# Second MLP layer of the last four token groups by Strassen's scheme, with gelu as one ScalarE instruction from group 7 on

## The chip, the cores and the metric

The kernel runs on one core of a Trainium2 chip. A core has five engines that run their own instruction streams in order and wait for each other on semaphores: TensorE (PE in the profile; its weight loads are shown apart as PEld), VectorE (DVE), ScalarE (ACT), GpSimd (POOL) and SyncE (SP), whose only work here is to issue transfers. The metric is the time of one execution on the device in microseconds. Before the change it is 345.12 us, the median of three runs (345.02 to 345.3).

## What is computed

An attention is followed by a two-layer MLP. For each of 8 batches and 8 heads there are 576 queries of 64 elements, and as many keys and values; 16 "beacon" keys and values stand before them. A query sees all beacon keys and, of the others, those up to its own place.

```
scores = 1/sqrt(64) * q @ concat(beacon_k, k).T     # causal mask on the k part
a      = softmax(scores)
attn   = a @ concat(beacon_v, v)
x      = attn, as 4608 tokens x 512                  # token = batch * 576 + place, heads side by side
h      = x @ w_in                                    # 512 x 2048
g      = h * sigmoid(1.702 * h)
out    = g @ w_out                                   # 2048 x 512, out is 4608 x 512 in float32
```

The kernel computes in float16 with float32 sums.

## The kernel before

**Attention.** The 64 pairs of batch and head are taken in 16 sets `s` of four heads of one batch (two sets a batch). `e_turn` (L353) brings q and k of a set into the layout in which the head's elements lie on the partitions, on VectorE. `e_qk` (L382) makes scores for a chunk of up to 512 columns for four heads at once, in a PSUM tile `s`; `e_exp` (L393) takes the exponential into the SBUF tile `E`; `e_mask` (L407 on VectorE, L414 on GpSimd) clears what is not seen; `e_zadd` (L445) adds up pieces of `E` for the row sums; `e_av` (L467) multiplies by the values, or by ones for the sums; `e_z1`, `e_z2` and `e_norm` (L478 to L496) divide and write `xT`, which here holds all 4608 tokens.

**MLP.** Tokens are cut into ten groups: groups 0 and 1 have 256 tokens, groups 2 to 9 have 512. In `e_m1` (L518) each of the 16 tiles of 128 columns of h takes four matmuls of 128x128 weights (of `w_in`) against the group's tokens, in one PSUM tile of a ring of four (`u0` to `u3`). `e_tanh` (L532, ScalarE) writes tanh(0.851 h) to `sig`, and `e_gate` (L539, VectorE) writes (sig + 1) * h to the tile `g`, which is twice the activation. In `e_m2` (L551) each of a group's four blocks of 128 tokens takes 16 matmuls, with a 128x128 block of `g` as the weights and 512 columns of `w_out` as the moving operand. `e_evac` (L565, ScalarE) halves the sum on its way to SBUF, and `e_store` (L571) writes 128 rows of 2 KB out from SP. The tile `g` has two buffers, so that the first layer of group g waits for the second layer of group g-2.

**Order.** Everything is issued in an order worked out ahead by `Plan` (L24): each piece of work is entered with an engine, an estimated duration, what it depends on, a priority `pr` (smaller first) and an earliest time `due`. `run` (L63) plays the engines forward and takes on each engine, but PE, the ready piece with the smallest (pr, ready time, sequence). On PE, `choose` (L137) takes scores first and then alternates first-layer and second-layer pieces, the lower group first. The engines then execute their streams in that order, whatever the real durations are. The chunks of scores are due at even distances between `T_ATT0` (11000 ns) and `T_ATT1` (245000 ns), so that MLP matmuls fill PE between them. A PSUM ring tile is free again when the piece that `closes` it is done (the gate for the first layer, the evacuation for the second).

Priorities on VectorE: exponent masks and divisions 0, gates 2, row-sum additions 3, transposes of q and k 4.

Of the kernel before, what the change touches and what calls it, by code (L numbers as in the profile page):

```python
# [162 lines left out]
def kernel(  # L163
# [37 lines left out]
    ep = ctx.enter_context(tc.tile_pool(name="ep", bufs=NE))  # L201
    zp = ctx.enter_context(tc.tile_pool(name="zp", bufs=2))
    gp = ctx.enter_context(tc.tile_pool(name="gp", bufs=2))
    sp = ctx.enter_context(tc.tile_pool(name="sp", bufs=3))
    pss = ctx.enter_context(tc.tile_pool(name="pss", bufs=1, space=bass.MemoryType.PSUM))
    psu = ctx.enter_context(tc.tile_pool(name="psu", bufs=1, space=bass.MemoryType.PSUM))
# [2 lines left out]
    ones = cst.tile([P, 32], F16, tag="ones", name="ones")  # L209
    w1t = cst.tile([P, NKT, DFF], F16, tag="w1", name="w1")  # L210
    w2t = cst.tile([P, NNT, DMODEL], F16, tag="w2", name="w2")
    xT = cst.tile([P, NKT, NTOK], F16, tag="xT", name="xT")
    bkf = cst.tile([P, NSET, D], F32, tag="bkf", name="bkf")
    bkn = cst.tile([P, 2, D], F16, tag="bkn", name="bkn")
    qn = [cst.tile([P, TR * D], F16, tag=f"qn{i}", name=f"qn{i}") for i in range(NB3)]
# [276 lines left out]

    def e_norm(s, x, half):
        b, hs = divmod(s, HS)
        t0 = b * S + half * HF
        nc.vector.tensor_tensor(  # L496
            out=xT[:, 2 * hs + x, t0 : t0 + HF],
            in0=rings[("av", s, x, half)][:, 0:HF],
            in1=zs[(s, half)][1][:, :],
            op=ALU.mult,  # L500
        )
# [7 lines left out]
    def e_m1(g, n0, n1):  # L509
        t0, t1 = GROUPS[g]  # L510
        w = t1 - t0
        if n0 == 0:
            gts[g] = gp.tile([P, NNT, 512], F16, tag="g", name="g")
        u = ring_tile(("m1", g, n0))
        for nt in range(n0, n1):
            o = (nt - n0) * w
            for kp in range(NKT):
                nc.tensor.matmul(  # L518
                    u[:, o : o + w],
                    w1t[:, kp, nt * P : (nt + 1) * P],  # L520
                    xT[:, kp, t0:t1],
                    start=(kp == 0),
                    stop=(kp == NKT - 1),
                )

    sigs = {}

    def e_tanh(g, n0, n1):
        w = (GROUPS[g][1] - GROUPS[g][0]) * (n1 - n0)
        sig = sp.tile([P, 512], F16, tag="sig", name="sig")  # L530
        sigs[(g, n0)] = sig
        nc.scalar.activation(  # L532
            out=sig[:, 0:w], in_=rings[("m1", g, n0)][:, 0:w], func=AFT.Tanh, scale=0.851
        )

    def e_gate(g, n0, n1):
        w = GROUPS[g][1] - GROUPS[g][0]
# [20 lines left out]

    osbs = {}

    def e_evac(g, mt, eng):
        osb = sp.tile([P, DMODEL], F32, tag="osb", name="osb")
        osbs[(g, mt)] = osb
        if eng == "ACT":
            nc.scalar.mul(out=osb[:, :], in_=rings[("m2", g, mt)][:, :], mul=0.5)  # L565
        else:
            nc.vector.tensor_scalar_mul(osb[:, :], rings[("m2", g, mt)][:, :], 0.5)

    def e_store(g, mt):
        t0 = GROUPS[g][0] + mt * P  # L570
        nc.sync.dma_start(out=out[t0 : t0 + P, :], in_=osbs[(g, mt)][:, :])  # L571


    T_ATT0, T_ATT1 = 11000, 245000
    NCH0 = 4 * HS
    T_CH = (T_ATT1 - T_ATT0) / (len(CHUNKS) - NCH0)

# [12 lines left out]
        return flight[-1]  # L590

    op = plan.op
    turn, qks, exps, masks, avs, norms = {}, {}, {}, {}, {}, {}
    vload = {}
    gates, m2s = {}, {}
# [35 lines left out]
    def turns(s):  # L631
        urgent = s < HS
        cast = op(
            "DVE", 80, ld_bk[s] + [turn.get((s - 2, 1))], lambda: e_bk(s),
            pr=0 if urgent else 4, due=max(8800 * s if s < HS else 26000, due_of(s) - 10000), name=f"bk{s}",
        )
        for which in (1, 0):
            deps = [ld_qk[(s, which)], cast if which else None]
            turn[(s, which)] = op(
                "DVE", 1095 + 140 * which, deps + [qks[i] for i in CH_OF.get(s - NB2, [])],  # L640
                lambda which=which: e_turn(s, which),
                pr=0 if urgent else 4, due=max(0, due_of(s) - 9000), name=f"turn{s}",
            )
# [35 lines left out]
    def values(s):  # L679
        b, hs = divmod(s, HS)  # L680
        whole = s >= ZSUM
        order = [(2, 1), (2, 0), (0, 0), (1, 0), (0, 1), (1, 1)] if whole else [
            (x, h) for h in range(2) for x in (2, 0, 1)
        ]
        sums, z2 = [], {}
        if whole:
            for i, w in enumerate((ZW, HF - s0s[2], HF, HF, S - s0s[3], S - s0s[4])):
                if i in (0, 2):
                    cols = [(ecol[i], ecol[i] + HF), (ecol[i + 1], ecol[i + 1] + HF)]
                    if i == 0:  # L690
                        cols = [(Z0, HF), (ecol[1], ecol[2])]
                    else:
                        cols = [(ecol[3], ecol[4]), (ecol[4], ecol[5])]
                else:
                    k = 2 if i == 1 else i + 2
                    cols = [(ecol[k], ecol[k] + w)]
                sums.append(
                    op(
                        "DVE", 80 + 0.55 * 4 * w, [x for u, v in cols for x in after(s, u, v)] + sums[-1:],
                        lambda i=i: e_zadd(s, i), pr=3, name="zadd",  # L700
                    )
                )
        for n, (x, half) in enumerate(order):
            deps = after(s, 0, ETOT) if whole else after(s, half * EHALF, ETOT if half else EHALF)
            if x < 2:
                deps += [vload[(b, j)] for (j, _, _) in AVP[half]] + [vload[(b, -1)]]
                deps += [z2[h] for h in range(2) if whole]
                deps += [avs[(s, 2, half)]]
            w = [e - a for (_, a, e) in AVP[half]]
            if x == 2 and whole:  # L710
                deps += sums
                w = [HF] if half else [ZW, Z0 - 32, 32]
            key = ("av", s, x, half)
            avs[(s, x, half)] = op(
                "PE", sum(y / 2.4 + 6 for y in w), deps,
                lambda x=x, half=half: e_av(s, x, half), kind="av",
                pr=(16 * s + (n if whole else 8 * half)) if s >= HS else half,
                ring=key, mode="c", name=f"av{s}.{x}.{half}", tail=w[-1],
            )
            if x == 2:  # L720
                z1 = op("DVE", 410, [avs[(s, x, half)]], lambda h=half: e_z1(s, h), pr=0, closes=key, name="z1")
                z2[half] = op("DVE", 600, [z1], lambda h=half: e_z2(s, h), pr=0, name="z2")
            else:
                norms[(s, x, half)] = op(
                    "DVE", 380, [avs[(s, x, half)], z2[half]], lambda x=x, half=half: e_norm(s, x, half),
                    pr=1 if s >= HS else 0, closes=key, name="norm",
                )
# [34 lines left out]
    for j in range(-1, NJ):  # L762
        load_v(1, j)

    def mlp(g):
        t0, t1 = GROUPS[g]
        w = t1 - t0
        xs = []
        for hb in range(t0 // HF, (t1 - 1) // HF + 1):
            b, half = divmod(hb, 2)  # L770
            for hs in range(HS):
                for x in range(2):
                    xs.append(norms[(HS * b + hs, x, half)])
        old = [m2s[(g - 2, mt, 3)] for mt in range((GROUPS[g - 2][1] - GROUPS[g - 2][0]) // P)] if g > 1 else []
        n = 512 // w
        for n0 in range(0, NNT, n):
            n1 = n0 + n
            key = ("m1", g, n0)
            pe = op(
                "PE", 4 * n * (w / 2.4 + 2.5), xs + w1_of[n0] + old, lambda n0=n0, n1=n1: e_m1(g, n0, n1),  # L780
                kind="m1", pr=g, ring=key, mode="m", name=f"m1.{g}.{n0}",
            )
            a = op("ACT", 555, [pe], lambda n0=n0, n1=n1: e_tanh(g, n0, n1), pr=1, name="tanh")
            gates[(g, n0)] = op(
                "DVE", 610, [a], lambda n0=n0, n1=n1: e_gate(g, n0, n1), pr=2, closes=key, name="gate"
            )
        for mt in range(w // P):
            key = ("m2", g, mt)
            prev = None
            for qt in range(4):  # L790
                deps = [gates[(g, n0)] for n0 in range(0, NNT if mt else 4 * qt + 4, n)] + [w2_ld[qt], prev]
                prev = op(
                    "PE", 4 * 215.8, deps, lambda g=g, mt=mt, qt=qt: e_m2(g, mt, qt), kind="m2",
                    pr=g, ring=key, mode="m", name=f"m2.{g}.{mt}.{qt}",
                )
                m2s[(g, mt, qt)] = prev
            ev = op("ACT", 560, [prev], lambda g=g, mt=mt: e_evac(g, mt, "ACT"), pr=1, closes=key, name="evac")
            op("SP", 60, [ev], lambda g=g, mt=mt: e_store(g, mt), name="store")

    g = 0  # L800
    for i, ch in enumerate(CHUNKS):
# [11 lines left out]
        for s, c0, c1 in ch:  # L813
            if c1 == ETOT:
                values(s)
                while s % HS == HS - 1 and g < NG and GROUPS[g][1] <= (s // HS + 1) * S:
                    mlp(g)
                    g += 1
    order = plan.run()
    for o in order:  # L820
        o.emit()
# [29 lines left out]
```

## Time and profile before

| what | value |
|---|---|
| median of the runs | 345.12 us |
| the profiled execution: its own time, and its span from first to last instruction | 345.13 us, 343.4 us |
| granted TensorE clock over the span | 1.000 |
| busy time of PE, DVE, ACT, POOL | 324.2, 234.3, 203.6, 117.2 us |
| last exponential (L393) starts, takes | 242.62 us, 1.88 us |
| first-layer matmuls (L518): first and last start | 18.2 us, 325.6 us |
| second-layer matmuls (L551): first and last start | 30.2 us, 339.4 us |
| the last evacuation (L565) starts, takes | 339.85 us, 0.60 us |

Times within the profile count from the start of the span. A group's row gives a number of instructions, their busy time and the mean duration of one, and the idle time before them with the engine that ended it. Matmuls overlap in their pipeline, so the pace of a stream of them is read from the starts, not from the duration of one. A row of the timeline gives a start, the time from that start to the end of the last merged instruction, and how many were merged ("x4"). A row of the windows gives busy time by engine in a stretch, and in brackets how many instructions.

### The profile page before, as it was taken

To read this page: it belongs to the slowest core of one execution; us is meant where nothing else is said; L and a number is where in the kernel's file an instruction comes from. 1 tells how busy PE (TensorE), PEld (TensorE's weight loads), DVE (VectorE), ACT (ScalarE), POOL (GpSimd) and SP (SyncE) were. 2 spreads that over 40 slices of the span, in tenths; PEclk is the share of its full clock that TensorE was granted. 3 is DMA by queue.
4 is the path that set the end of the run, shared out by engine and by line. 5 is a ranking of instruction groups with operands and counts; after the bars stand their busy time and mean duration, and the time that the engine had idled before them with its cause. 6 is when DMAs were issued, how large, how long until landed. Compare 5 with 4: busy or idle time off the path is not lost.

```text
span 343.4 us, 9569 instructions
## 1 busy us (share of the span) xinstructions
PE 324.2 (94%) x4104; PEld 172.7 (50%) x4104; DVE 234.3 (68%) x454; ACT 203.6 (59%) x247; POOL 117.2 (34%) x190
## 2 busy tenths in 40 slices
PE   0699899999999999999999999999999999999995
PEld 0476666544554554555454545555444544444442
DVE  3856878499968798998888987987546444444400
ACT  1575587788547775776777676676643444444411
POOL 8765583394256329212653182231100000000000
PEclk9999999999999999999999999999999999999999
DMA  7999999694339149805093396000000000100021
GB/s 128 170 205 209 190 209 110 133 69 74 48 116 142 33 71 87 118 32 103 5 161 64 79 92 111 32 33 34 31 31 32 32 31 31 62 32 31 32 82 71
DMA packets 54122, 28.80 MB, mean 84 GB/s; under 512 B 41280, under 2 KB 45376, under 8 KB 54080
## 3 DMA queue, kind: packets, MB, share of 16 engines
q0 software_dynamic: 47552, 18.49, 46.0%
q1 hardware_dynamic: 6464, 9.69, 7.9%
q8 instruction: 32, 0.52, 0.6%
q14 instruction: 10, 0.08, 0.1%
q10 hardware_dynamic: 64, 0.01, 0.0%
HBM read 37.22 MB, written 9.44 MB: 136 GB/s over the span
## 4 chain that ended last, share of the span: by engine, by line
PE 75%; DVE 11%; issue 5%; POOL 3%; ACT 3%; DMA 2%; SPq 1%; DVEq 0%; POOLq 0%; ACTq 0%
PE u L551 33%; PE u L518 28%; PE u L467 7%; PE s L382 7%; ACT E L393 3%; DVE g L539 3%; DVE zs L445 2%; POOL E L414 2%; DMA bkf<-in_beacon_k_dram 2%; DVE qT L353 1%; DVE kT L353 1%; POOL vb L313 1%; DVE rz L487 1%; DVE zt L478 1%; DVE xT L496 1%
## 5 line engine op out<-in xcount | busy, mean ns | idle before, releaser
L518 PE MATMUL u<-xT,w 128*128 128x512 f16 (+1 forms) x640 | 145.7, 360 | 2.4 <-DVE g L539 1.1
L551 PE MATMUL u<-w,g 128*128 128x512 f16 x576 | 142.5, 379 | 0.0
L539 DVE SCALAR_TENSOR_TENSOR g<-sig,u 128x512 f16<-128x512 f16 x144 | 96.6, 681 | 64.0 <-ACT sig L532 63.2
L532 ACT ACTIVATE sig<-u 128x512 f16<-128x512 f32 x144 | 85.2, 598 | 86.5 <-PE u L518 84.0
L393 ACT ACTIVATE E<-s 128x2048 f16<-128x2048 f32 (+4 forms) x66 | 98.8, 1515 | 26.0 <-PE s L382 25.2
L414 POOL TENSOR_SCALAR_AFFINE_SELECT E<-E 128x512 f16<-128x512 f16 (+3 forms) x90 | 52.8, 612 | 118.3 <-ACT E L393 107.3
L518 PEld LDWEIGHTS <-w 128*128 128x128 f16 x640 | 60.7, 98 | 62.1 <-issue 2.9
L551 PEld LDWEIGHTS <-g 128*128 128x128 f16 x576 | 54.5, 98 | 63.4 <-issue 0.2
L382 PE MATMUL s<-qT,kT 32*128 32x32 f16 (+9 forms) x1544 | 36.0, 227 | 12.2 <-DVE qT L353 10.9
L382 PEld LDWEIGHTS <-kT 32*128 32x128 f16 x1544 | 28.5, 95 | 33.8 <-issue 21.4
L565 ACT ACTIVATE osb<-u 128x512 f32<-128x512 f32 x36 | 21.5, 597 | 22.3 <-PE u L551 22.3
L445 DVE TENSOR_TENSOR zs<-zs,E 128x192 f16<-128x192 f16 (+3 forms) x48 | 27.0, 563 | 4.6 <-ACT E L393 2.7
L467 PE MATMUL u<-E,vb 128*32 128x288 f16 (+4 forms) x1024 | 29.2, 258 | 0.8 <-DVE g L539 0.4
L496 DVE TENSOR_TENSOR xT<-u,rz 128x288 f16<-128x288 f32 x64 | 26.2, 448 | 4.1 <-PE u L467 3.7
L313 POOL DMA_DIRECT2D vb<-in_v_dram x32 | 27.2, 863 | 2.1 <-DMA qn<-in_q_dram 1.4
L467 PEld LDWEIGHTS <-vb 128*32 128x32 f16 (+1 forms) x1024 | 22.6, 98 | 4.6 <-issue 1.9
L353 DVE STREAM_TRANSPOSE kT<-kn 128x576 f32<-128x576 f32 x16 | 20.1, 1257 | 3.8 <-DMA kn<-in_k_dram 2.8
L353 DVE STREAM_TRANSPOSE qT<-qn 128x576 f32<-128x576 f32 x16 | 20.0, 1247 | 0.5 <-DMA qn<-in_q_dram 0.5
L445 DVE TENSOR_TENSOR zs<-E 128x704 f16<-128x704 f16 (+1 forms) x24 | 16.1, 671 | 5.4 <-POOL E L414 3.4
L478 DVE STREAM_TRANSPOSE zt<-u 128x288 f32<-128x288 f32 x32 | 14.0, 463 | 5.6 <-PE u L467 5.6
L487 DVE STREAM_TRANSPOSE rz<-rc 128x288 f32<-128x288 f32 x32 | 15.3, 478 | 1.1
L297 POOL DMA_DIRECT2D kn<-in_k_dram x16 | 9.1, 569 | 2.8 <-DVE g L539 2.0
(27 smaller groups left out, 66.8 us busy)
## 6 DMA issues: line engine op xcount, KB each, us to landing
out_dram<-osb SPq DMA_DIRECT2D x36, 256.0 KB, 2.0
kn<-in_k_dram POOLq DMA_DIRECT2D x16, 288.0 KB, 6.7
qn<-in_q_dram POOLq DMA_DIRECT2D x16, 288.0 KB, 6.3
vb<-in_v_dram POOLq DMA_DIRECT2D x24, 128.0 KB, 5.9
w<-in_moe_w_in_dram POOLq DMA_DIRECT2D x8, 256.0 KB, 9.0
w<-in_moe_w_out_dram POOLq DMA_DIRECT2D x4, 512.0 KB, 13.9
vb<-in_v_dram POOLq DMA_DIRECT2D x8, 112.0 KB, 3.3
vb<-in_v_dram POOLq DMA_DIRECT2D x8, 80.0 KB, 5.3
```

Source lines behind the costliest of these rows:

```text
L313: nc.gpsimd.dma_start(out=t[0 : hi - lo, j, h0:h1, :], in_=v[b, h0:h1, lo:hi, :].rearrange("h n d -> n h d"),)
L353: nc.vector.transpose(out=f32(dst.rearrange("p n e -> p (n e)")).rearrange("p (r t) -> p t r", t=TR), in_=f32(src[:, :]).rearrange("p (t c ...
L382: nc.tensor.matmul(sc[:, h, o : o + w], kT[s % NB2][r : r + 32, j * P : (j + 1) * P, d], qT[s % NB2][r : r + 32, a : a + w, d], start=(d = ...
L393: nc.scalar.activation(out=Es[s][:, :, c0:c1], in_=ss[i][:, :, o : o + c1 - c0], func=AFT.Exp, scale=0.125,)
L414: nc.gpsimd.affine_select(out=blk, in_=blk, compare_op=ALU.is_ge, fill=0.0, base=off + (Nb if j == 0 else 0), pattern=[[0, Q], [1, w]], ch ...
L445: nc.vector.tensor_tensor(out=t[:, :, o : o + w], in0=x, in1=y, op=ALU.add)
L467: nc.tensor.matmul(u[32 * h : 32 * h + 32, a:e], lhs, src[0:kw, h, col : col + e - a], start=first, stop=last,)
L496: nc.vector.tensor_tensor(out=xT[:, 2 * hs + x, t0 : t0 + HF], in0=rings[("av", s, x, half)][:, 0:HF], in1=zs[(s, half)][1][:, :], op=ALU. ...
L518: nc.tensor.matmul(u[:, o : o + w], w1t[:, kp, nt * P : (nt + 1) * P], xT[:, kp, t0:t1], start=(kp == 0), stop=(kp == NKT - 1),)
L532: nc.scalar.activation(out=sig[:, 0:w], in_=rings[("m1", g, n0)][:, 0:w], func=AFT.Tanh, scale=0.851)
L539: nc.vector.scalar_tensor_tensor(out=gts[g][:, n0:n1, 0:w], in0=sigs[(g, n0)][:, 0 : n * w].rearrange("p (n w) -> p n w", n=n), scalar=1.0 ...
L551: nc.tensor.matmul(o[:, :], gts[g][:, nt, mt * P : (mt + 1) * P], w2t[:, nt, :], start=(nt == 0), stop=(nt == NNT - 1),)
```

## The change

The change has five parts.

1. **Second layer of groups 6 to 9.** The product of a group, 512 tokens x 2048 by 2048 x 512, is taken as a product of 2 x 2 blocks (tokens in halves of 256, the 2048 in halves of 1024, output columns in halves of 256), by Winograd's form of Strassen's scheme: seven block products in place of eight. `e_prod` makes one of them: 8 x 2 matmuls of 128x128 weights against 256 columns, both token blocks in the halves of one ring tile, entered in four pieces of four matmuls.
2. **Sums on VectorE.** Four sums of blocks of `g` (`e_s`: three into the new tiles `sA`, one in place in `g`), each in four pieces of 128x512 elements of float16, wait for the gates (or gelus) they read and for all products of the group before, and have priority 2. Four sums of blocks of `w_out` (`e_t`, 128x2048 each, priority 3, from 200 us on) are made once; the fourth goes into the memory of `bkf`, after the last beacon key was read from it. The seven products are put together by one scaling on ScalarE (`e_half`) and seven instructions `e_join` on VectorE, and written out by four stores of 256 rows x 1 KB (`e_store4`).
3. **Gelu.** From group 7 on, one ScalarE instruction with the function `Gelu_apprx_sigmoid` takes the place of tanh and gate. The first one waits for all exponentials and for group 6's tanhs, the others wait for the first. These groups' outputs are not halved.
4. **`xT` as a ring** of 4 x 576 tokens in place of 4608. Values of a batch wait for the first layer of the groups whose places they overwrite; group 5 lies over the ring's end, and its first layer is issued in two parts of 256 tokens.
5. **Plan.** `T_ATT0`, `T_ATT1` become 13000 and 235000 ns. Output tiles come from a pool of their own, of four.

```diff
-    xT = cst.tile([P, NKT, NTOK], F16, tag="xT", name="xT")
+    XR = 4 * S
+    NPL, NPE, GEL = 6, 10, 7
+    HM, HN = 256, NNT // 2
+    xT = cst.tile([P, NKT, XR], F16, tag="xT", name="xT")
+    sA = [cst.tile([P, HN, HM], F16, tag=f"sA{i}", name=f"sA{i}") for i in range(3)]
+    tB = [cst.tile([P, HN, HM], F16, tag=f"tB{i}", name=f"tB{i}") for i in range(3)]
...
+            cut = max(t0, t1 // XR * XR)
+            for a, e in ((t0, cut), (cut, t1)):
+                for kp in range(NKT if a < e else 0):
+                    nc.tensor.matmul(
+                        u[:, o + a - t0 : o + e - t0],
+                        w1t[:, kp, nt * P : (nt + 1) * P],
+                        xT[:, kp, a % XR : (e - 1) % XR + 1],
...
+    def e_gelu(g, n0, n1):
...
+        nc.scalar.activation(
+            out=gts[g][:, n0:n1, 0:w],
+            in_=rings[("m1", g, n0)][:, 0 : n * w].rearrange("p (n w) -> p n w", n=n),
+            func=AFT.Gelu_apprx_sigmoid,
+        )
...
-    T_ATT0, T_ATT1 = 11000, 245000
+    def e_prod(g, p, n0, n1):
+        u = ring_tile(("p", g, p))
+        w = lambda i, j: w2t[:, HN * i : HN * (i + 1), HM * j : HM * (j + 1)]
+        lhs, rhs = {
+            1: (quarter(g, 0, 0), w(0, 0)),
+            2: (quarter(g, 0, 1), w(1, 0)),
+            3: (sA[2], w(1, 1)),
+            4: (quarter(g, 1, 1), tb(2)),
+            5: (sA[0], tb(0)),
+            6: (sA[1], tb(1)),
+            7: (quarter(g, 1, 0), tb(3)),
+        }[p]
+        for n in range(n0, n1):
+            for mt in range(2):
+                nc.tensor.matmul(
+                    u[:, HM * mt : HM * (mt + 1)],
+                    lhs[:, n, mt * P : (mt + 1) * P],
+                    rhs[:, n, :],
...
+    def e_join(g, p, src, dst):
...
+        nc.vector.scalar_tensor_tensor(
+            out=osbs[(g, dst)][:, :], in0=rings[("p", g, p)][:, :], scalar=scale_of(g), in1=osbs[(g, src)][:, :],
+            op0=ALU.mult, op1=ALU.add,
+        )
...
+    T_ATT0, T_ATT1 = 13000, 235000
...
+    SQ, SDVE, TDUE = 2, 0, 200000
+
+    def weights():
+        prev = []
+        for i in range(4):
+            prev = [op("DVE", 1450, w2_ld + prev, lambda i=i: e_t(i, "DVE"), pr=3, due=TDUE, name="t")]
+            tds[i] = prev[0]
...
+    def products(g):
+        eng = "POOL" if g < SDVE else "DVE"
+        sd = {}
+        for n0 in range(0, HN, SQ):
+            n1 = n0 + SQ
+            prev = []
+            for i in range(4):
+                deps = prev + done.get(g - 1, [])
+                for n in range(n0, n1):
+                    deps += [gates[(g, n)], gates[(g, n + HN)]]
...
+                o = op(
+                    "PE", 2 * SQ * 109, deps, lambda n0=n0: e_prod(g, p, n0, n0 + SQ), kind="m2", pr=g,
+                    ring=("p", g, p), mode="m", name=f"m2.{g}.{p}.{n0}",
+                )
...
+        prod(1)
+        half = op("ACT", 560, [last[1]], lambda: e_half(g, 1, "m"), pr=1, closes=("p", g, 1), name="half")
+        prod(2)
+        c11 = join(2, "m", "a", [half])
+        store(c11, "a", 0, 0)
+        prod(6)
+        u2 = join(6, "m", "m", [c11])
+        prod(7)
+        u3 = join(7, "m", "u", [u2])
+        prod(4)
+        c21 = join(4, "u", "b", [u3])
+        store(c21, "b", 1, 0)
+        prod(5)
+        u4 = join(5, "m", "m", [u3], False)
+        c22 = join(5, "u", "u", [c21, u4])
+        store(c22, "u", 1, 1)
+        prod(3)
+        c12 = join(3, "m", "m", [u4])
+        store(c12, "m", 0, 1)
...
+    for o in gelus[:1]:
+        for d in exps.values():
+            also(o, d)
+    for o in gelus[1:]:
+        also(o, gelus[0])
```

## The prediction

> **What bounds the kernel now.** I read the busy windows first, to see which engine is full in which stage. These are seven stretches of the span, in the order PE, PEld, DVE, ACT, POOL, then clock, DMA share and GB/s.
>
> ```profile
> 20.00:60.00 40.00, 38.41 (x745) 26.91 (x744) 30.10 (x59) 28.34 (x31) 23.56 (x39) 1.00 1.32 184
> 60.00:120.00 60.00, 59.09 (x893) 31.44 (x893) 49.01 (x98) 43.63 (x48) 29.89 (x47) 1.00 0.64 88
> 120.00:180.00 60.00, 58.63 (x866) 31.02 (x865) 53.08 (x106) 41.98 (x48) 26.11 (x43) 1.00 0.62 82
> 180.00:240.00 60.00, 60.00 (x869) 31.42 (x867) 50.92 (x101) 40.45 (x46) 20.68 (x33) 1.00 0.38 64
> 240.00:300.00 60.00, 60.00 (x378) 27.94 (x377) 28.60 (x48) 26.84 (x43) 1.49 (x3) 1.00 0.09 36
> 300.00:343.40 43.40, 39.76 (x185) 17.80 (x182) 11.01 (x16) 14.33 (x24) 0.00 (x0) 1.00 0.13 49
> ```
>
> From 20 us on TensorE is full at full clock: it stands idle for 1.6 + 0.9 + 1.4 = 3.9 us up to 180 us, and not at all from there to the last 3.6 us. Until 240 us VectorE is full too, to some 85%. After 240 us every engine but TensorE is at most half busy, so there a matmul saved is time saved. A busy PE is only worth something if it streams at its pace, so I looked next at the order of time on PE, at the end and in an early place where 256-column matmuls run.
>
> ```profile
> 324.06 1.03 PE L551 MATMUL u<-w,g 128*128 128x512 f16 x4
> 324.92 1.03 PE L518 MATMUL u<-xT,w 128*128 128x512 f16 x4
> 325.79 13.98 PE L551 MATMUL u<-w,g 128*128 128x512 f16 x64
> ```
>
> ```profile
> 26.31 0.27 PE L518 MATMUL u<-xT,w 128*128 128x256 f16 x1
> 26.52 0.54 PE L382 MATMUL s<-qT,kT 32*128 32x192 f16 x24
> 26.99 2.79 PE L518 MATMUL u<-xT,w 128*128 128x256 f16 x24
> ```
>
> The 64 matmuls of the last group take 13.98 us from first start to last end; one of them lasts 0.38 us, so the pace is (13.98 - 0.38) / 63 = 0.2159 us. Units of four start 0.86 us apart, which is the same pace: changing between the layers costs nothing. The 24 matmuls of 256 columns, three pieces, go at (2.79 - 0.27) / 23 = 0.1096 us, boundaries of pieces included.
>
> **The saving on TensorE.** A group's second layer now is 64 x 0.2159 = 13.82 us. After the change it is 7 products x 16 matmuls = 112 x 0.1096 = 12.27 us. Four groups: 4 x 1.55 = **6.2 us** less. The first layer of group 5 is cut into 128 matmuls of 256 columns: 128 x 0.1096 - 13.82 = **+0.2 us**. Every 256-column matmul brings its own weights, and here a rule speaks against the change. The Trainium skill, "TensorE: Matmul & The Clock Gate", Part 3, section "The mechanism", says that a weight load runs beside a matmul only where the two use different row groups; these use all rows. With the mean of the weight-load rows, 98 ns, in series, a product would take 112 x (0.1096 + 0.098) = 23.3 us against 64 x (0.2159 + 0.098) = 20.1 us: 3.2 us a group lost. The row decides: those 24 matmuls each have a weight load of 128 columns, and their pace leaves no place for one. I take 0.1096. What could expose one is a piece that really waits for a semaphore: 0 to 0.1 us for each of 4 x 28 pieces. The waits should be over long before, so I take **+0.1 us**.
>
> **VectorE from 200 to 240 us.** This is the one stage where the change adds work to a full engine.
>
> ```profile
> sum 40.00, PE 40.00 PEld 21.28 DVE 33.39 ACT 26.17 POOL 14.04; mean PE 10.00 PEld 5.32 DVE 8.35 ACT 6.54 POOL 3.51
> ```
> ```profile
> 208.16 0.52 DVE L445 TENSOR_TENSOR zs<-E 128x704 f16<-128x704 f16 x1
> 209.01 0.76 DVE L445 TENSOR_TENSOR zs<-E 128x1152 f16<-128x1152 f16 x1
> 163.52 2.00 DVE L445 TENSOR_TENSOR zs<-zs,E 128x1152 f16<-128x1152 f16 x2 [1.73 <-ACT E L393]
> ```
>
> Two-input float16 additions cost 0.52 us for 704 elements and 0.76 for 1152, so 0.54 ns an element and 0.14 fixed. A sum of `w_out` (2048) is 1.2 us, four are 4.9 us. Of the 33.4 us in this stretch 10.1 us are gates (the windows for tile `g`); the rest, 23.3 us, is attention, and that is packed tighter, from 234 to 222 us for the same chunks: x 1.054 = 24.5 us. Together 10.1 + 24.5 + 4.9 = 39.5 of 40 us: just full. While GpSimd masks, a 1152-addition took about 1 us or more (the last row above); at 1.6 times the price the weight sums are 7.9 us and the stage overruns by 2.5 us. What is late then: the transposes and row sums behind (priorities 4 and 3), then scores, exponentials, and the gelu that waits for them all. The cover is the distance of that gelu. Before, the last exponential ended at 242.62 + 1.88 = 244.5 us, just when TensorE came to group 7. The matmuls ahead of group 7 stay as they are, so TensorE still comes there at about 243 us, and the exponentials are due 10 us earlier. Cover: some 8.5 us. On the other side, the tighter pacing shifts every chunk against the MLP pieces and may add to, or close, the 3.9 us of idle: bounds -2 and +3 us. I take **+0.3 us**, near nothing, since TensorE took no harm at VectorE's 53.08 of 60 us between 120 and 180 us beyond 1.4 us.
>
> **VectorE and ScalarE after 240 us.** Per group the gates go (16 x 0.60 = 9.7 us, start to start); 16 sums of 512 elements come (0.42 us each, about 0.34 start to start, 5.4 us) and seven joins, which like the gate read PSUM (0.68 us, 0.60 start to start, 4.2 us). 9.6 against 9.7 us: the load stays, at half of the time. Sums of group g wait for the products of g-1; before they are needed, products 1 and 2 run, which take none of them, 8 pieces between 8 first-layer units: 8 x (0.44 + 0.86) = 10.4 us, against 5.4 us of sums. That is cover enough. In group 9 no first layer runs beside: 3.5 us of cover, then product 6 needs the second sum (8 of 16 sums, 2.7 us), product 7 the fourth (5.4 us plus two joins, 6.6 us, for its last piece, which TensorE would reach at 6.5 us). I take **+0.1 us**, bounds 0 and 1.8. Gelu replaces tanh at the same shape; no row shows it. The nearest is tanh, 598 ns; that the function costs more is bounded by the cover: a unit comes every 1.3 us.
>
> The gelu needs another function table. The row is the one table load at the start, 1283 ns. The Trainium skill, "ScalarE: Activation LUTs", section "What ACT_TABLE_LOAD costs", adds about 1.38 us of drain, 2.66 us for a switch. The PSUM tile of the first unit would be held 0.86 + 0.27 + 1.28 + 0.60 = 3.0 us by the row, 4.4 us by the page. Three more ring tiles take in first-layer units 1.3 us apart, one of them being used by a product; the cover is some 3.9 us. By the row it costs nothing, by the page 0.5 us. I take the row, **0**, as ScalarE has an idle 1.1 us before a unit in which to load.
>
> **The end.** After the last matmul 3.6 us remain.
>
> ```profile
> 339.85 0.60 ACT L565 ACTIVATE osb<-u 128x512 f32<-128x512 f32 x1 [2.86 <-PE u L551]
> 340.47 0.33 SPq L571 DMA_DIRECT2D out_dram<-osb  x1
> ```
>
> A join (0.69 us) stands in the place of the evacuation (0.60): **+0.1 us**. The store has the same 256 KB in runs of 1 KB in place of 2 KB; it landed in 2.0 us. Bounds 0 and +1; **+0.1 us**. The stores before it are hidden, the queue is nearly idle. The `xT` ring costs nothing where values find the first layer done: batch 7 writes over group 5, whose last gate here is at 200 us, while its values would start at about 217 us.
>
> **Sum.** -6.2 + 0.2 + 0.1 + 0.3 + 0.1 + 0.1 + 0.1 = -5.3 us. The profiled execution had 343.4 us of span and 1.7 us around it, 345.13 in all, which is the median; so **339.8 us**.
>
> **Rivals.** *VectorE takes part of it back.* The overrun of 2.5 us, or idle added by the pacing up to 3 us, comes through to TensorE: 341.5 to 344 us, 342.4 in the middle. For it: 39.5 of 40 us. Against it: the 8.5 us of cover.
>
> *The pacing closes idle time.* Up to 2 us of the 3.9 us go: 337.8 us. For it: the idle is there. Against it: no edit aims at one of these places.
>
> *Slower, by the wait of the first gelu.* All of TensorE stops when four ring tiles are full and an exponential is still missing. It decides when the last exponential ends more than 8.5 + 5.3 + 0.7 = 14.5 us behind its due place, after some 249 us. Then I expect around 252 us, 3 us over that point: 345.8 + 3 = 349 us. It takes VectorE's backlog of 2.5 us to grow sixfold, by a transpose held up behind sums and gates in each of the last sets; against it, a chunk ahead of its due time catches up.
>
> *The change doesn't do what it says.* Products stop for their sums, 1.5 us a group: 345 us. Only group 9 has cover that thin.
>
> **Numbers.** About 0.2%, 0.7 us, is what a measurement of this kernel tells from no change. Chances: the forecast 0.68, with its own range 338.6 to 341.3; the part taken back 0.17; pacing gain 0.06; no change 0.03; slower 0.06. Faster by over 0.2%: 0.68 + 0.17 + 0.06 = 0.91; within: 0.03; slower: 0.06. The range of 8 in 10 leaves out the slower case, no change, the upper part of the part taken back and the lower half of the pacing gain: 338.2 to 342.6 us.
>
> **What would show it.** In the changed profile: 112 matmuls of a product group at 0.110 us, also where units alternate (4 take 0.44 us); PE idle from 180 us to the end of matmuls under 0.5 us; the last exponential at about 235 us and the first gelu at about 244 us; the end of matmuls 3.6 to 3.9 us before the span's end; group 6's gates and the sums not waiting for more than 2 us. I am wrong if PE waits for VectorE around 240 us, if the pace in products is over 0.115 us, or if the idle before 180 us has changed by over 2 us.

## The result, and the profile after

The changed kernel takes 341.44 us, the median of four runs (341.31 to 341.8), beside 345.21 us of the kernel before: a ratio of 0.9893, with a 95% interval of 0.9876 to 0.991. That is 3.8 us saved, where 5.3 were forecast (339.8 us, range 338.2 to 342.6). The time lies inside the range, 0.1 us above the forecast's own part of it (338.6 to 341.3). The profiled execution has a span of 339.7 us, 3.7 us less.

The busy windows of the changed kernel, in the columns PE, PEld, DVE, ACT, POOL, clock, DMA share, GB/s, show at once where the missing part went:

```profile
20.00:60.00 40.00, 37.65 (x755) 26.18 (x744) 30.16 (x58) 28.47 (x31) 25.06 (x43) 1.00 1.35 188
60.00:120.00 60.00, 56.66 (x859) 29.78 (x857) 51.56 (x100) 42.16 (x48) 28.75 (x47) 1.00 0.60 80
120.00:180.00 60.00, 59.87 (x917) 33.67 (x917) 52.58 (x105) 42.63 (x48) 26.66 (x41) 1.00 0.63 86
180.00:240.00 60.00, 60.00 (x920) 35.55 (x918) 55.18 (x106) 41.23 (x48) 21.57 (x34) 1.00 0.37 62
240.00:300.00 60.00, 60.00 (x465) 38.86 (x464) 27.35 (x66) 23.99 (x40) 0.00 (x0) 1.00 0.12 40
300.00:339.70 39.70, 35.83 (x274) 26.50 (x271) 18.23 (x41) 9.80 (x17) 0.00 (x0) 0.99 0.16 54
```

TensorE is idle for 2.35 + 3.34 + 0.13 = 5.8 us between 20 and 180 us, where it was 3.9 before. After 180 us it is full, as before, up to the last 3.9 us. So this loss lies long before the first product, which starts at 244.05 us, in a part of the attention that the change seems not to touch.

The products themselves are as forecast. The order of time on PE around the first of them, then at the end of the last group:

```profile
245.79 0.60 PE L640 MATMUL u<-w,g 128*128 128x256 f16 x4
246.22 1.03 PE L526 MATMUL u<-xT,w 128*128 128x512 f16 x4
...
323.44 3.66 PE L640 MATMUL u<-w,g 128*128 128x256 f16 x32
...
333.92 1.91 PE L640 MATMUL u<-w,sA 128*128 128x256 f16 x16
```

A piece of four takes 0.43 to 0.44 us from its start to the next unit's. Group 9's 112 matmuls run from 323.44 to 335.83 us, the end of the last line; less the last one's 0.27 us that is 12.12 / 111 = 0.1092 us each, with no stop. PE ends there too; the span ends 3.9 us later, against 3.6 before (the store in runs of 1 KB lands in 2.2 us, the one of 2 KB in 2.0).

ScalarE at the first gelu:

```profile
243.39 0.60 ACT L584 ACTIVATE osb<-u 128x512 f32<-128x512 f32 x1 [0.27 <-PE u L571]
244.00 1.28 ACT L547 ACT_TABLE_LOAD   x1
245.30 1.29 ACT L547 ACTIVATE g<-u 128x512 f16<-128x512 f32 x2
```

The table load takes 1.28 us, the gelu starts 0.02 us after it, and a gelu takes 597 ns by its group's row. TensorE does not notice: its lines above follow without a gap.

### The profile page after: what moved, and what is told of

Read it like the earlier page. It is cut to its first block, busy times and chain, and to the rows that moved or that the text cites. A ratio compares the mean times of both kernels' runs of the same rounds, so it can differ in the third digit from the quotient of the medians.

```text
span 339.7 us, 10091 instructions
## 1 busy us (share of the span) xinstructions
PE 318.0 (94%) x4360; PEld 196.9 (58%) x4360; DVE 246.8 (73%) x502; ACT 196.7 (58%) x236; POOL 117.5 (35%) x190
## 4 chain that ended last, share of the span: by engine, by line
PE 79%; DMA 9%; DVE 7%; POOL 2%; issue 1%; ACT 0%; DVEq 0%; POOLq 0%
PE u L526 32%; PE u L571 19%; PE u L640 14%; PE u L473 8%; PE s L388 7%; DMA w<-in_moe_w_in_dram 5%; DMA w<-in_moe_w_out_dram 4%; DVE g L559 2%; DVE zs L451 2%; DVE osb L656 1%; DVE xT L502 1%; DVE rz L493 1%; POOL vb L319 1%; POOL E L420 0%; ACT E L399 0%
## 5 line engine op out<-in xcount | busy, mean ns | idle before, releaser
L526 PE MATMUL u<-xT,w 128*128 128x512 f16 (+1 forms) x704 | 147.7, 341 | 1.2 <-DVE zt L484 0.5
L526 PEld LDWEIGHTS <-w 128*128 128x128 f16 x704 | 66.3, 98 | 48.6 <-issue 1.3
L540 ACT ACTIVATE sig<-u 128x512 f16<-128x512 f32 x96 | 57.2, 598 | 45.2 <-PE u L526 42.4
L571 PE MATMUL u<-w,g 128*128 128x512 f16 x320 | 81.5, 380 | 0.4 <-DMA w<-in_moe_w_out_dram 0.3
L559 DVE SCALAR_TENSOR_TENSOR g<-sig,u 128x512 f16<-128x512 f16 x96 | 64.3, 678 | 20.6 <-ACT sig L540 20.2
L656 DVE SCALAR_TENSOR_TENSOR osb<-u,osb 128x512 f32<-128x512 f32 x28 | 18.9, 690 | 48.1 <-PE u L640 37.1
L547 ACT ACTIVATE g<-u 128x512 f16<-128x512 f32 x48 | 28.7, 597 | 43.1 <-PE u L526 43.0
L640 PEld LDWEIGHTS <-sA 128*128 128x128 f16 x192 | 18.8, 98 | 4.7
```

The lines of the kernel that those rows point to most:

```text
L526: nc.tensor.matmul(u[:, o + a - t0 : o + e - t0], w1t[:, kp, nt * P : (nt + 1) * P], xT[:, kp, a % XR : (e - 1) % XR + 1], start=(kp == 0) ...
L540: nc.scalar.activation(out=sig[:, 0:w], in_=rings[("m1", g, n0)][:, 0:w], func=AFT.Tanh, scale=0.851)
L559: nc.vector.scalar_tensor_tensor(out=gts[g][:, n0:n1, 0:w], in0=sigs[(g, n0)][:, 0 : n * w].rearrange("p (n w) -> p n w", n=n), scalar=1.0 ...
L571: nc.tensor.matmul(o[:, :], gts[g][:, nt, mt * P : (mt + 1) * P], w2t[:, nt, :], start=(nt == 0), stop=(nt == NNT - 1),)
L640: nc.tensor.matmul(u[:, HM * mt : HM * (mt + 1)], lhs[:, n, mt * P : (mt + 1) * P], rhs[:, n, :], start=(n == 0 and mt == 0), stop=(n == H ...
```

## The experiments

**Due times, products and gelu, each alone.** There were two theories for the 1.9 us of new idle: *pacing* (the tighter due times of the scores) and *other edits* (the ring of `xT`, prices in the plan, and what else came along). Two more runs size the products and the gelu. First the changed kernel with the old due times:

```diff
-    T_ATT0, T_ATT1 = 13000, 235000
+    T_ATT0, T_ATT1 = 11000, 245000
```

> The changed kernel with the old due times of the scores, T_ATT0 and T_ATT1 at 11000 and 245000 ns. Theory 'pacing' (the tighter due times cost the 2.2 us of TensorE idle that the changed kernel has more between 20 and 120 us): that idle falls back from 5.7 us to about 3.5, the last exponential ends at about 244.5 us, TensorE comes to group 7 about then, and the time is 339.3 us, or up to 340.6 if the first gelu is waited for. Rival 'other edits' (ring of xT, changed prices in the plan, group 5 in two parts): the idle stays, 341.4 us, or more with the wait for the gelu.

Measured: 340.87 us, 0.6 us less than the change. Neither number came out. The idle from 20 to 180 us is 1.38 + 3.56 + 0.31 = 5.3 us: most of it is still there.

```profile
20.00:60.00 40.00, 38.62 (x796) 27.12 (x789) 30.26 (x59) 28.79 (x31) 24.66 (x42) 1.00 1.32 184
60.00:120.00 60.00, 56.44 (x835) 29.53 (x828) 49.43 (x98) 42.23 (x48) 28.17 (x45) 1.00 0.63 84
120.00:180.00 60.00, 59.69 (x894) 33.28 (x893) 51.46 (x104) 40.88 (x48) 26.22 (x42) 1.00 0.62 86
```

In the kernel before, the same edit the other way:

```diff
-    T_ATT0, T_ATT1 = 11000, 245000
+    T_ATT0, T_ATT1 = 13000, 235000
```

> The kernel before with the new due times alone, 13000 and 235000 ns. Theory 'pacing': 2.2 us more idle of TensorE between 20 and 120 us, 347.4 us. Rival 'other edits': 345.2 us.

Measured: 346.30 us beside 345.08, ratio 1.0033 (1.002 to 1.0046). In this kernel pacing costs 1.2 us, not 2.2. It is a part of the cause and not all of it.

Next the old second layer in all groups, with the rest of the change kept:

```diff
-    NPL, NPE, GEL = 6, 10, 7
+    NPL, NPE, GEL = 10, 10, 7
```

> The changed kernel with the old second layer (64 matmuls of 512 columns) in all groups; gelu, xT ring and pacing stay. Both theories give the saving of the products alone: 4 x 1.55 = 6.2 us, so 341.4 + 6.2 = 347.6 us, with the same idle before 120 us. If the sums on VectorE took part of the saving back before 240 us, less: 346 us or under.

Measured: 347.62 us (the edit also puts the first-layer units of groups 6 to 9 back in their old order, which the change had altered for the products). Against 341.44 the products are worth **6.2 us**, as worked out, so the sums on VectorE take nothing of it back that this difference could show. And 347.6 us without products, beside 345.08 of the kernel before, says that all else in the change together costs 2.5 us.

Then the products with tanh and gate in all groups:

```diff
-    NPL, NPE, GEL = 6, 10, 7
+    NPL, NPE, GEL = 6, 10, 10
```

> The changed kernel with tanh and gate in all groups. Theory 'TensorE bound, gelu only takes load off VectorE': VectorE has 9.7 + 5.4 + 4.2 = 19.3 us of work in a group's 26 us, so 341.4 us, at most 0.7 more at the last group. Rival 'gelu is needed to keep the products fed': TensorE waits for VectorE after 240 us, 343 us or more.

Measured: 343.04 us, 1.6 us more than with gelu; the rival's number (343 or more) came out. Its profiled execution had a granted clock of 0.96 between 20 and 60 us, and from there to the first product each matmul starts 2.0 us later than in the changed kernel; so I use only what waits after 240 us. The order of time on PE:

```profile
250.50 0.31 PE L473 MATMUL u<-zs,ones 128*32 128x288 f16 x4
251.31 0.26 PE L473 MATMUL u<-zs,ones 128*32 128x176 f16 x4 [0.50 <-ACT osb L651]
...
255.61 1.47 PE L640 MATMUL u<-tB,sA 128*128 128x256 f16 x12 [0.24 <-DVE g L559]
```

and VectorE just before, where the gates of group 7 and the sums of group 6 take turns:

```profile
245.78 1.42 DVE L591 TENSOR_TENSOR sA<-g 128x512 f16<-128x512 f16 x4
247.12 0.75 DVE L591 TENSOR_TENSOR sA<-sA,g 128x512 f16<-128x512 f16 x2
247.79 0.68 DVE L559 SCALAR_TENSOR_TENSOR g<-sig,u 128x512 f16<-128x512 f16 x1
248.39 0.75 DVE L591 TENSOR_TENSOR sA<-sA,g 128x512 f16<-128x512 f16 x2
```

TensorE is idle 0.75 us between 250 and 260 us, where it is full with gelu. Such idle understates a stop, since the busy time of the last matmul reaches into it: at the first wait 0.81 us pass between the starts, at the second some 0.4 us more than the 0.86 of a unit. VectorE is busy for 8.9 of these 10 us, with gelu for 3.4. The mean load of 19.3 in 26 us that I reckoned with hides this burst: all 16 sums become ready at once, when the group before is done, and gates with the same priority queue among them. The shorter wait is ended by a gate. The longer one is ended by ScalarE's scaling of product 1 (`e_half`, L651); that late gates stand behind that one too is not shown.

**The price in the plan.** What is left of *other edits* is small before 120 us: no product, no gelu, no sum, no wait of the ring exists there yet. But the order can differ. PE's order of time at 20 us, first in the kernel before, then in the changed one, shows that it does:

```profile
19.98 0.83 PE L382 MATMUL s<-qT,kT 32*128 32x208 f16 x32
20.75 2.79 PE L518 MATMUL u<-xT,w 128*128 128x256 f16 x24
23.47 0.53 PE L382 MATMUL s<-qT,kT 32*128 32x288 f16 x24
```

```profile
19.69 0.55 PE L388 MATMUL s<-qT,kT 32*128 32x208 f16 x32 [0.41 <-ACT E L399]
20.16 2.01 PE L526 MATMUL u<-xT,w 128*128 128x256 f16 x16
22.11 0.54 PE L388 MATMUL s<-qT,kT 32*128 32x288 f16 x24
```

Three first-layer units before the next scores have become two. The one edit that bears on this is a constant, which the list of the change's parts above does not name: the plan's price of a first-layer unit, `4 * n * (w / 2.4 + 2.5)`, has `2.8` in the change. For a unit of this group (two column tiles of 256 tokens) that is 875.7 in place of 873.3 ns. When the kernel before is issued, `Plan.run` has PE free after the second unit at 21307.7 ns of its own time, and the next scores ready at 21309.2 ns: 1.5 ns too late, so a third unit goes first. With 2.8 in it PE is free at 21314.9 ns and the scores are ready at 21311.6 ns, so the scores go first. Every later decision follows from that. So I tested the constant alone, in both kernels and with both pacings.

```diff
-                "PE", 4 * n * (w / 2.4 + 2.5), xs + w1_of[n0] + old, lambda n0=n0, n1=n1: e_m1(g, n0, n1),
+                "PE", 4 * n * (w / 2.4 + 2.8), xs + w1_of[n0] + old, lambda n0=n0, n1=n1: e_m1(g, n0, n1),
```

> The kernel before, with only the plan's price of a first-layer matmul changed from w/2.4 + 2.5 ns to w/2.4 + 2.8 ns, as the change has it. Nothing but the order of issue can differ. Theory 'price' (this price makes the plan choose scores before or after a first-layer unit otherwise, 21 us into the plan, and all that follows is another order, with more idle of TensorE): the idle between 20 and 180 us rises from 3.9 us to that of the changed kernel with old due times, 1.4 + 3.6 + 0.3 = 5.3 us, and the time to 346.5 us. Rival 'other edits' (ring of xT, output buffers, waits that came with them): 345.1 us.

> The kernel before with both: the price of 2.8 ns and the due times 13000 and 235000 ns. Theory 'price and pacing': idle between 20 and 180 us as in the changed kernel, 2.4 + 3.3 + 0.1 = 5.8 us, 347.3 us (the changed kernel without its products, 347.6, less 0.2 for group 5 in two parts). Rival 'other edits': as with the new due times alone, 346.3 us.

Measured: 346.76 us for the price alone (ratio 1.0053, 1.0038 to 1.0068), 347.67 us for both, beside 345.03. A constant that no engine ever sees costs 1.7 us. In the windows of the kernel before with the price alone, the idle is nearly that of the changed kernel with old due times, 1.2 + 3.6 + 0.3 us:

```profile
20.00:60.00 40.00, 38.76 (x778) 26.90 (x776) 30.58 (x59) 28.69 (x31) 24.47 (x41) 1.00 1.32 186
60.00:120.00 60.00, 56.41 (x823) 29.26 (x816) 49.51 (x99) 42.31 (x48) 27.97 (x45) 1.00 0.63 84
120.00:180.00 60.00, 59.69 (x873) 31.34 (x872) 51.49 (x105) 40.94 (x48) 26.26 (x43) 1.00 0.63 86
```

The price and the pacing together, without any of the change's other parts, reach the 347.6 us of the changed kernel without products. The traces agree: up to about 171 us, where group 5 comes in two parts, the 2596 matmuls of this kernel and of the change stand in the same order by kind and size, and the idle from 20 to 180 us is 5.8 us in both. So nothing of that idle is left for the ring or for the output buffers to explain. Then the other way, in the changed kernel:

> The changed kernel with the price at 2.5 ns and the due times of 11000 and 245000 ns, so that its order is that of the kernel before for some 207 us. Theory 'price and pacing': 345.1 - 6.2 + 0.2 = 339.1 us, up to 0.5 us more if the first gelu, which now has no distance from the last exponential, holds TensorE up. Rival 'other edits': 340.9 us, as with the old due times alone.

> The changed kernel with the price at 2.5 ns and its own due times. Theory 'price and pacing': the early order is that of the kernel before with new due times, 346.3 - 6.2 + 0.2 = 340.3 us. Rival 'other edits': 341.4 us.

Measured: **339.69 us** with both old values (ratio 0.9843, 0.9828 to 0.9858) and 339.86 us with the old price and the new due times (0.9852, 0.9837 to 0.9867). Both beat the change as it was made. So in the changed kernel price and pacing together cost 1.8 us, not the 2.6 of the kernel before; nearly all of it is the price (1.6 us with the new due times), and the due times cost 0.6 us with the new price and 0.2 with the old. The first is 0.6 us above the 339.1 us of the theory, but far from the rival's 340.9. TensorE's busy time in the three windows from 20 to 180 us is that of the kernel before to 0.03 us. The last exponential ends at 244.8 us and the first gelu starts at 246.1 us, yet TensorE stays full from 240 to 300 us, so it is not the gelu; some 0.3 us are the longer end. The profiled execution is the one of 339.27 us; the 0.4 us by which the three others are longer lie in no trace, and stay open.

Which wait TensorE meets in the worse order is on its list of waits (us in total, times, longest). In the changed kernel, then in the kernel before, between 88 and 103 us:

```profile
PE u L473 <- DVE g L559: 2.0, 4, 1.0
PE u L473 <- DVE zs L451: 0.5, 1, 0.5
```

```profile
PE u L467 <- DVE g L539: 0.3, 1, 0.3
```

The row sums and values of the attention need a tile of the PSUM ring, the ring's tiles are closed by gates, and the gates stand in VectorE's queue behind transposes, divisions and additions. The first of the four waits, in the changed kernel:

```profile
90.03 0.52 DVE L451 TENSOR_TENSOR zs<-E 128x704 f16<-128x704 f16 x1
90.46 0.67 DVE L559 SCALAR_TENSOR_TENSOR g<-sig,u 128x512 f16<-128x512 f16 x1
91.19 0.26 PE L473 MATMUL u<-zs,ones 128*32 128x176 f16 x4 [0.58 <-DVE g L559]
```

**How much room VectorE has.** I had put the weight sums between 200 and 240 us at nothing, with 8.5 us of cover up to the first gelu.

```diff
-            prev = [op("DVE", 1450, w2_ld + prev, lambda i=i: e_t(i, "DVE"), pr=3, due=TDUE, name="t")]
+            prev = [op("DVE", 1450, w2_ld + prev, lambda i=i: [e_t(i, "DVE") for _ in range(2)], pr=3, due=TDUE, name="t")]
```

> The changed kernel with each of the four sums of w_out made twice over (same result, same place in the order): 5.3 us more on VectorE between 203 and about 215 us, where it has 0.4 of 20 us idle from 200 to 220 us and 3.0 of 20 us from 220 to 240 us. Theory 'cover' (late gates and transposes there are taken up by the PSUM ring and by the distance of the first gelu): TensorE stays full, 341.4 to 341.9 us. Rival 'VectorE is the bound there': most of 5.3 us comes through, 344 us or more.

> The same four times over: 15.9 us more on VectorE, each sum holding up the gate behind it by 3.7 us more. Theory 'cover': the ring of four tiles covers some 2 to 3 us of a late gate, so each of the four sums costs TensorE 1 to 1.5 us, 346 us. Rival 'VectorE is the bound there': 15.9 us less the 3.4 us that it has idle up to 240 us, 354 us.

Measured: 346.10 us twice over and 358.06 us four times over. Of 5.3 us more, 4.7 come through by these medians; of 15.9 us, 16.6. Twice over, eight executions with a mean granted clock of 0.998 or more took 344.9 to 345.7 us, and eight with 0.995 or less 346.5 to 347.8, so a part of the 4.7 us goes with the clock; at full clock it is 3.7. My theory of a cover fell, and even the rival's 354 us was too low. One of the reasons is in the windows of the kernel with four: where TensorE stands most, its granted clock is lower, 0.70 in this stretch (the column after POOL) and 0.83 between 230 and 240 us.

```profile
210.00:220.00 10.00, 7.25 (x62) 2.85 (x55) 9.79 (x12) 2.55 (x3) 0.00 (x0) 0.70 0.01 2
```

PE's order of time with the sums twice over, and VectorE's just before:

```profile
219.36 1.03 PE L526 MATMUL u<-xT,w 128*128 128x512 f16 x4
221.89 1.02 PE L571 MATMUL u<-w,g 128*128 128x512 f16 x4 [1.50 <-DVE g L559]
```

```profile
218.61 2.63 DVE L591 TENSOR_TENSOR bkf<-w 128x2048 f16<-128x2048 f16 x2
221.16 0.68 DVE L559 SCALAR_TENSOR_TENSOR g<-sig,u 128x512 f16<-128x512 f16 x1
```

The next second-layer piece waits for a gate held up behind a weight sum; at 209 us it is the same, with a wait of 0.97 us. The last exponential ends at 241.0 us and the first gelu starts at 249.5 us, so the distance of 8.5 us is still unused; it covers nothing, since TensorE meets VectorE much earlier. Told of the longer sums, the plan does better (with a price of 2900 ns its order ends in a deadlock and gives no time, so the price is 2700):

```diff
-            prev = [op("DVE", 1450, w2_ld + prev, lambda i=i: [e_t(i, "DVE") for _ in range(2)], pr=3, due=TDUE, name="t")]
+            prev = [op("DVE", 2700, w2_ld + prev, lambda i=i: [e_t(i, "DVE") for _ in range(2)], pr=3, due=TDUE, name="t")]
```

> The sums of w_out made twice over, and the plan told a price of 2700 ns in place of 1450 (two sums take 2.45 to 2.9 us), so that it orders the other work around them. Theory 'VectorE is the bound in that stage': it has 3.4 us idle from 200 to 240 us in the changed kernel and gets 5.3 us more, so some 2 us come through whatever the order, 343.4 us. Rival 'the 4.7 us came from an order that didn't know of the longer sums': TensorE finds other work, 341.4 to 342 us.

Measured: 343.64 us (342.5 to 344.4), so 2.5 of the 4.7 us were the order. The other 2.2 us are the number of the theory, but not its mechanism. From 200 to 240 us, first in the profile of this kernel (an execution of 342.54 us at full clock), then in that of the change:

```profile
sum 40.00, PE 40.00 PEld 21.20 DVE 37.52 ACT 25.96 POOL 11.08; mean PE 10.00 PEld 5.30 DVE 9.38 ACT 6.49 POOL 2.77
```

```profile
sum 40.00, PE 40.00 PEld 22.05 DVE 36.62 ACT 27.25 POOL 9.71; mean PE 10.00 PEld 5.51 DVE 9.16 ACT 6.81 POOL 2.43
```

TensorE is full in both; even with the sums doubled VectorE is not the bound there, once the order fits. What the 2.2 us are stays open: the two executions at full clock are 1.1 us above the change, and the four with a mean granted clock of 0.994 or 0.995 another 1 to 2 us. In the change as made the sums cost TensorE nothing in that stage; the plan's price for them, 1.45 us, was fair (they took 1.42, 1.22, 1.48 and 1.21 us).

**One piece in place of four.**

```diff
-    SQ, SDVE, TDUE = 2, 0, 200000
+    SQ, SDVE, TDUE = 8, 0, 200000
```

> The changed kernel with each sum of g in one piece of 2048 elements, and each product in one piece of 16 matmuls, in place of four pieces. VectorE's fixed part falls from 4 to 1 in a sum: 16 x 0.34 = 5.4 us becomes 4 x 1.15 = 4.6 us a group. Theory 'sums are covered': 341.4 us, in group 9 the second sum is there after 2.3 us and the fourth after 4.6 us, as before. Rival 'the pieces matter': product 6 of a group can't start on the first piece, and TensorE stops in group 9 and at group 6, 342.5 us or more.

Measured: 342.17 us (341.77 to 344.12), 0.7 us more, little above the scatter. The profiles differ by as much, and not by the rival's mechanism: TensorE ends at 335.69 us, no later than with four pieces. The end is what differs. The row of the last joins, first of this kernel, then of the change:

```profile
333.98 3.21 DVE L656 SCALAR_TENSOR_TENSOR osb<-u,osb 128x512 f32<-128x512 f32 x5 [2.15 <-PE u L640]
```

```profile
333.24 3.31 DVE L656 SCALAR_TENSOR_TENSOR osb<-u,osb 128x512 f32<-128x512 f32 x5 [2.35 <-PE u L640]
```

Product 7 needs the fourth sum. In one piece it stands behind products 4 and 5, five joins hang on it, and they run in one row at the end. With small pieces product 7 mixes with product 5 and ends 0.7 us earlier, so that the five joins end at 336.55 us, about when a single join after the last matmul would have ended (335.83 + 0.69 us).

## Why the prediction was right, and which term was off

The saving came as it was worked out, and the loss beside it was a term taken at near nothing. That the time still fell into the range is in part luck: the range had room for idle added by the pacing, while most of that loss came from a price that the prediction does not mention.

**The products: right.** Forecast 6.2 us, measured 6.2 (347.62 - 341.44). The pace of 0.1096 us read from the first layer of the 256-token groups held at 0.1092, in pieces of four between other units. The 0.1 us for exposed weight loads was not needed. The rule of the Trainium skill, "TensorE: Matmul & The Clock Gate", Part 3, section "The mechanism", that a weight load runs beside a matmul only on other row groups, would have made the change a loss; the measurement decides against it here. The same section also has a load pulled ahead when it goes to the background weight buffer, and the measured pace fits that.

**Pacing and idle: mis-sized, and for another reason.** This is the term that was off: "I take +0.3 us, near nothing". In the kernel before it measured 2.6 us with its companion (347.67 - 345.03), 1.2 us for the due times alone and 1.7 us for the price; in the changed kernel 1.8 us for both (341.44 - 339.69). The bounds of -2 and +3 us held. The sign of being wrong that was set for it, an idle before 180 us changed by over 2 us, was missed narrowly: it rose from 3.87 to 5.82 us. Two things were wrong in the argument. It rested on VectorE's load between 120 and 180 us, where the idle even fell to 0.13 us, while the waits came earlier, most of them between 60 and 120 us, where the new order let gates pile up. And it weighed only the due times; the change also moved a price by 0.3 ns a matmul, which has no effect on the chip except through the order.

**VectorE from 200 to 240 us: right in the sum, wrong in the reason.** No loss was forecast and none came. The load was 36.6 us, not 39.5. The gates are not fewer: 17 start there, before 15. It is the attention that was put too high: with the same due times, but without products and their sums, the whole stretch has 33.2 us of VectorE, no more than the 33.4 before, so the tighter pacing did not pack it by the factor 1.054. And the 8.5 us up to the first gelu (the last exponential ended at 236.8 us) were no cover, as the doubled sums show.

**After 240 us: right for the change, wrong for the gelu.** TensorE is full, group 9 does not stop, gelu costs 597 ns. "The load stays" missed that gelu does more than balance the sums: without it 1.6 us are lost, at least in part to a gate late in a burst.

**The table load: right, the row held.** The Trainium skill, "ScalarE: Activation LUTs", section "What ACT_TABLE_LOAD costs", adds a drain of 1.38 us to the load; here the gelu starts 0.02 us after the load ends, and the measurement decides.

**The end: right in size, by another path.** +0.2 us was forecast, 3.9 us against 3.6 came. But not one join stands there: five in a row do, and they end about when one after the last matmul would have.

The account by runs: +2.6 us for price and pacing (345.03 to 347.67), nothing measurable for the ring, the output tiles, group 5 in two parts and gelu together (347.67 to 347.62), -6.2 for the products (347.62 to 341.44). The +0.2 us for group 5 was not measured alone. Of the 2.6 us the windows show 1.9 as idle; where the rest lies is not shown, but idle understates stops. The parts do not add in every order: with old price and old due times the rest of the change saves 5.3 us (345.03 - 339.69), 0.9 less than the products alone in the new order.

Of the rivals, the slower one never came near: its mechanism needs the gelu to be held, and the last exponential ended 8.5 us ahead of it. The measured time lies just under the lower edge (341.5 us) of "VectorE takes part of it back", which named idle from the pacing and gave it up to 3 us. Its other half, an overrun from 200 to 240 us, did not occur.

## What to carry to other kernels

Where an order of issue is computed from prices, a change of any price or due time is a change of the whole kernel: compare with the old kernel under the new prices first, and look for the first instruction that stands elsewhere in the order, before explaining a loss by the new work. Cover is to be read next to the place where work is added: which piece behind it does the full engine need next, and not how far away the last consumer is. A mean load well under the stage's length doesn't exclude a burst where many pieces become ready on one event.

## What the runs showed of the hardware

A matmul of 256 columns with weights of its own costs half of one of 512 (0.1092 and 0.2159 us) also when pieces of four alternate with others, although its weight load alone lasts 98 ns. A float16 addition of 512 elements takes 0.42 us by its row, and four in a row 1.43 us, so they start 0.34 us apart; one of 2048 takes between 1.21 and 1.48 us in the same stage. With the weight sums four times over, TensorE waited for VectorE for 2.4, 2.8 and 3.8 us at a time; the granted clock was 0.70 and 0.83 of full speed in two stretches of 10 us around these waits, and full again from 240 us on. With the sums twice over, the profiled execution kept 1.00 through waits of up to 1.5 us, though eight of the kernel's 16 executions had a mean of 0.995 or less; and without gelu the profiled execution had 0.96 between 20 and 60 us, with no wait above 1.0 us there. So these runs give no rule. A switch of ScalarE's table costs the 1.28 us of the load and nothing visible beside it.
